# An attention kernel on one core: constants made between the evictions of x, and a tail whose banks are waited for singly

## The chip, the cores and the metric

The kernel runs on one core of one Trainium2 chip. A core has a matrix engine (TensorE; PE in the profile, PEld for its weight loads), a vector engine (VectorE, DVE), an activation engine (ScalarE, ACT), a general engine (GpSimd, POOL), a queue engine that here only issues DMAs (SyncE, SP), and 16 DMA engines. Each engine works through its own list of instructions in order, and waits on semaphores for the others. TensorE writes its results to PSUM, a memory of eight banks of 128 x 512 fp32; an "eviction" is the instruction that copies such a result to SBUF, the working memory.

The metric is the time of one execution on the device, in microseconds (us), taken as the median of several runs.

## The reference

Two attentions over the same x (1 x 2048 x 640, bf16) are mixed by a gate. Each has its own weights, 32 heads of 20 columns, and its own output projection.

```python
q, k, v = (x @ wqkv) split into 3 x 32 heads x 20
# A: full attention
p = softmax(q @ k.T * 20 ** -0.5)          # 2048 x 2048 for each head
a = (p @ v) @ wo
# B: each position sees itself and 7 earlier ones, 2 apart
logits = (q[s] . k[s - 2 * w]) * 20 ** -0.5   for w in 0..7, masked where s - 2 * w < 0
b = (softmax(logits) . v[s - 2 * w]) @ wo_B
g = sigmoid((x * gate_w).sum(-1))
out = g * a + (1 - g) * b
```

The exponentials of A, 32 x 2048 x 2048, are the bulk of the work.

## The kernel before

**Tiling.** Heads are taken in fours ("q" counts 8 groups of four heads), positions of the query in four chunks of 512 ("qc"). A unit is one head, one block of 128 keys and 512 queries: TensorE multiplies a slice of `kT` with `qT` into one PSUM bank (L1731), ScalarE takes the exponential of two or three banks at once into `ebuf` (L1756), and TensorE multiplies that with v into the bank `obank` (L1801). Some units go to VectorE instead, which makes powers of two by integer arithmetic (L1745, L905). Beside this stream run generators for all else: projections of q, k, v for the later heads, attention B, the gate, the output projection ("fold").

**What sets the order.** The kernel's text is a planner. Every call `T(engine, cost, instruction, reads, writes)` puts one instruction at the end of that engine's list, notes what it must wait for from the buffers it reads and writes, and advances a modelled clock for that engine, `sch.avail`. A generator is given its turn when the modelled clocks and free banks allow it. So the order of the body depends on those modelled clocks; at the end of the head they are set to fixed numbers (L1548). When the list of every engine is complete the instructions are emitted with their semaphores.

**The head** (about the first 18 us) is written out by hand, in this order:

1. Constants: an iota on GpSimd (L518); on VectorE `idf`, the difference of column and row index (L523, in the tile `rB`), the identity (L524), zeroed tiles (L534 to L542). GpSimd clears `vA` and five `qT` tiles (L527, L544).
2. x comes in four blocks of 512 rows by DMA. `turn` (L1400) transposes a block on TensorE into PSUM. `x_out` evicts it to `xT`: ScalarE takes two fifths (L1413), VectorE three (L1416).
3. On GpSimd, `w_pad` (L598) spreads the first weights of k into `kvw` once they have landed, an iota (L1472) writes the input of a later mask, and `kt_fill` (L1465) fills `kT` for groups 1 to 3 with a pattern read from the two-element tile `ones2`. Then come the first weights of q (L598 into `WqP`) and one more fill.
4. `k_first` (L1423) projects the first four heads' k for a block of 512 positions into a bank; `k_max` (L1437, VectorE) takes the largest |k| of it, and `k_out` (L1444, ScalarE) evicts it. The fourth block is projected in two halves (L1497), has its maxima taken in two (L1514) and is evicted in one piece by ScalarE (L1525). From the maxima VectorE makes `KM` (in the tile `eB`, L1520).
5. The first q is projected in two halves (L1497). |q| of the first half is made by ScalarE (L1517), of the second by VectorE (L1522). A matmul of |q| with `KM` (L1531) adds an upper bound of the scores, and VectorE writes both halves of `qT` from PSUM (L1535, twice). Then the first scores can be multiplied.

The blocks are interleaved on each engine's list as the calls of the module's end part stand: turn 0, x_out 0, turn 1, x_out 1, k_first 0, turn 2, k_max 0, k_out 0, x_out 2, k_first 1, turn 3, k_max 1, x_out 3, k_out 1, k_first 2, k_max 2, then the halves.

**The generator `constants()`** makes, after the head and between evictions of v, the following on VectorE: `KMd`, a mask for sums of |k| (three instructions, L554, L555, L557, from the iota of L1472), and `Rep`, a matrix that adds up heads: a copy of the identity (L562) and six additions `Rep = (idf == shift) + Rep` (L565), each of which reads the SBUF tiles `idf` and `Rep` and waits for the one before. `Rep` is needed by attention B only, `KMd` by the bounds of later heads.

**The tail** (`tail()`) is written by hand too. For the last 512 rows, four blocks of 128, part of the output projection has been summed up ahead. Columns 512 to 639 of all four blocks lie in a bank called the strip; columns 0 to 511 of blocks 2 and 3 in two "tail banks", those of blocks 0 and 1 in the two halves of `score[0]`. The last head's matmuls (L1212) go to the strip, block 2, block 3, block 0, block 1. VectorE adds the strip to what was summed before (L1234), ScalarE evicts blocks 2 and 3 (L1240), VectorE adds blocks 0 and 1 (L1243), and each block is written to memory by one DMA (L1248), those of blocks 2 and 3 issued from ScalarE, those of 0 and 1 from SyncE.

## Time and profile before

| | |
|---|---|
| median of 3 runs | 790.83 us (790.80 to 791.33) |
| profiled execution | 791.24 us, span of its instructions 789.4 us |
| TensorE clock granted | 1.000 |
| ScalarE busy in the span | 769.0 us (97%) |
| TensorE busy | 752.3 us (95%) |
| VectorE busy | 721.5 us (91%) |
| GpSimd busy | 123.9 us (16%) |
| first exponential begins | 18.22 us |
| busy before 18.2 us | TensorE 15.79, VectorE 13.45, GpSimd 9.81, ScalarE 8.39 us |
| busy from 784.5 us on | VectorE 1.88, ScalarE 1.09, TensorE 0.71 us |

The span runs from the first to the last instruction in the trace; the execution's time has 1.84 us more around it. A row of the page reads: line of the kernel, engine, operation, output tile <- input tiles, shapes, how often; after the bar the busy time, the mean duration in ns of one, and the idle time of the engine just before these instructions, with what ended that idle time. In the rows in order of time the first two columns are start and duration in us, and the bracket at the end is idle time before, with what ended it. Where several of one kind follow each other they share a row, "x3".

### The profile page before, as it was taken

What the parts mean: (1) busy time and instruction counts of PE and PEld (TensorE: products, weight loads), DVE (VectorE), ACT (ScalarE), POOL (GpSimd) and SP (SyncE); (2) the same over time, 40 slices, a digit from 0 to 9 for tenths busy, and PEclk for the clock granted to TensorE, in tenths of its full rate; (3) what the DMA queues carried; (4) which work ended last, traced back from release to release, by engine and by line L of the source; (5) the groups of instructions that cost most, each with busy time, mean ns of one, the idle gap of its engine ahead of it and who ended that gap; (6) DMA issues with size and microseconds to landing.
All of it is one profiled execution on the core that took longest, in us unless ns stands there. A gap on an engine that the chain in (4) does not pass through costs nothing.

```text
span 789.4 us, 29584 instructions
## 1 busy us (share of the span) xinstructions
PE 752.3 (95%) x12556; PEld 290.6 (37%) x12556; DVE 721.5 (91%) x1282; ACT 769.0 (97%) x732; POOL 123.9 (16%) x230
## 2 busy tenths in 40 slices
PE   8999999999999999999999999999999999999997
PEld 5423333232233334333334433434443433344323
DVE  7798888999999989999988999998999999898894
ACT  4999999999999999999999999999999999999996
POOL 4011202111112011111111101111111111111210
PEclk9999999999999999999999999999999999999999
DMA  7241121010021123130111312012113013100311
GB/s 227 62 109 25 40 44 33 14 24 18 8 71 30 41 42 73 24 72 16 23 40 42 76 41 58 14 41 71 25 31 71 26 24 71 46 7 7 74 31 40
DMA packets 62663, 36.16 MB, mean 46 GB/s; under 512 B 26884, under 2 KB 61972, under 8 KB 62532
## 3 DMA queue, kind: packets, MB, share of 16 engines
q1 hardware_dynamic: 62244, 33.94, 17.9%
q8 instruction: 100, 1.64, 0.9%
q10 hardware_dynamic: 288, 0.33, 0.1%
q14 instruction: 31, 0.25, 0.1%
HBM read 12.85 MB, written 3.54 MB: 21 GB/s over the span
## 4 chain that ended last, share of the span: by engine, by line
PE 43%; ACT 26%; DVE 17%; issue 11%; SPq 2%; DMA 1%; POOL 0%; DVEq 0%; ACTq 0%
ACT ebuf L1756 25%; PE score L1731 13%; PE obank L1801 12%; PE side L632 12%; DVE uD L1745 6%; DVE eD L905 4%; PE score L632 2%; DVE kvw L1092 1%; SPq L975 1%; DVE qkvB L967 1%; DMA oTd<-in_A_x_dram 1%; PE obank L1822 1%; PE score L1822 1%; PE side L1003 1%; DVE kvw L993 1%
## 5 line engine op out<-in xcount | busy, mean ns | idle before, releaser
L1756 ACT ACTIVATE ebuf<-score 128x1024 bf16<-128x1024 f32 (+1 forms) x699 | 757.0, 1266 | 4.4 <-PE score L1731 3.7
L1745 DVE TENSOR_SCALAR uD<-score 128x512 int16<-128x512 f32 x392 | 260.2, 680 | 14.7 <-PE score L1731 13.3
L1731 PE MATMUL score<-qT,kT 32*128 32x512 bf16 x1856 | 253.8, 384 | 17.7 <-ACT ebuf L1756 13.6
L905 DVE TENSOR_SCALAR eD<-uD 128x2048 int16<-128x2048 int16 x294 | 195.0, 687 | 4.5 <-PE obank L1801 3.4
L1801 PE MATMUL obank<-ebuf,vA 128*21 128x512 bf16 x1656 | 153.5, 385 | 1.7 <-DVE oTt L865 0.6
L1731 PEld LDWEIGHTS score<-qT,kT 32*128 32x128 bf16 x1856 | 63.0, 91 | 211.6 <-ACT ebuf L1756 147.4
L925 POOL TENSOR_TENSOR vS<-vA,vw 128x252 bf16<-128x252 bf16 x98 | 59.9, 613 | 388.5 <-DVE eD L905 252.8
L1801 PE MATMUL obank<-eD,vS 128*21 128x512 bf16 x1176 | 103.5, 379 | 0.0
L632 PE MATMUL side<-xT,wBs 128*32 128x256 bf16 x2400 | 93.6, 280 | 2.2 <-DVE oB L1125 0.7
L632 PEld LDWEIGHTS side<-xT,wBs 128*32 128x32 bf16 x2400 | 68.1, 141 | 27.9 <-issue 14.5
L1801 PEld LDWEIGHTS obank<-ebuf,vA 128*21 128x21 bf16 x1656 | 36.0, 89 | 83.0 <-issue 56.4
L1092 DVE TENSOR_TENSOR kvw<-kvw,eB 128x2048 bf16<-128x2048 bf16 x40 | 48.1, 1214 | 0.2 <-DMA kvw<-qkvB 0.2
L993 DVE TENSOR_TENSOR kvw<-qkvB 128x2048 bf16<-128x2048 bf16 x40 | 48.0, 1215 | 0.1
L882 POOL TENSOR_TENSOR oN<-oTt,rcp 128x256 bf16<-128x256 f32 x62 | 38.8, 625 | 58.0 <-DVE eD L905 39.5
L967 DVE CAST qkvB<-side 128x512 bf16<-128x512 f32 (+1 forms) x72 | 42.0, 593 | 4.5 <-PE side L632 4.3
L873 POOL TENSOR_TENSOR rcp<-rcp,gA 128x16 f32<-128x16 f32 x31 | 9.1, 292 | 192.0 <-DVE eD L905 90.9
L1801 PE MATMUL obank<-uD,vA 128*21 128x512 bf16 x392 | 38.1, 379 | 0.0
L1801 PEld LDWEIGHTS obank<-eD,vS 128*21 128x21 bf16 x1176 | 28.8, 91 | 19.8 <-issue 2.0
L1731 PE MATMUL score<-woBp,kT 32*128 32x512 bf16 x192 | 30.0, 384 | 1.8 <-ACT ebuf L1756 1.6
L632 PE MATMUL side<-xT,kvw 128*32 128x512 bf16 (+1 forms) x360 | 30.1, 382 | 0.6 <-DVE vA L833 0.3
L632 PE MATMUL side<-kvw,xT 128*32 128x160 bf16 (+1 forms) x740 | 28.5, 263 | 1.3 <-DVE vA L833 0.5
L865 DVE STREAM_TRANSPOSE oTt<-obank 128x512 f32<-128x512 f32 x32 | 22.6, 707 | 6.5 <-PE obank L1801 6.5
(194 smaller groups left out, 555.8 us busy)
## 6 DMA issues: line engine op xcount, KB each, us to landing
kvw<-qkvB SPq DMA_DIRECT2D x128, 80.6 KB
wBs<-in_B_wqkv_dram SPq DMA_DIRECT2D x15, 160.0 KB
WqP<-in_A_wqkv_dram SPq DMA_DIRECT2D x14, 160.0 KB
oTd<-oN SPq DMA_DIRECT2D x108, 20.0 KB
out_dram<-outsb SPq DMA_DIRECT2D x12, 160.0 KB
qT<-dst SPq DMA_DIRECT2D x93, 20.0 KB
kvw<-in_A_wqkv_dram SPq DMA_DIRECT2D x2, 800.0 KB
oTd<-in_A_x_dram SPq DMA_DIRECT2D x2, 640.0 KB
```

Of the source, the lines that this page charges most:

```text
L632: ins = e.matmul(o[j:k, :], l(j) if callable(l) else l[:, j:k], r, start=(first and i == 0), stop=(last and i == n - 1), skip_group_check= ...
L865: T("dve", 0.625, lambda e: e.transpose(oTt[:, :], obank[:, :]), reads=["obank"], writes=["oTt"])
L882: T(en, c2 if n == 4 else 0.56, lambda e, oo=oo, ii=ii, ib=ib: e.tensor_tensor(oo, ii, ib, ALU.mult), reads=["rcp", "oTt"], **{"accum" if ...
L905: T("dve", 0.065 + 0.1334 * n, lambda e, k=k, sl=sl: e.tensor_scalar(eD[:, sl % NS, 0:512 * n].bitcast(I16), uD[d % 2][:, 0:512 * n].bitca ...
L925: T("pool", 0.607, lambda e: e.tensor_tensor(vS[:, d % 2, :, :], _ap(vA, (kb * NQ + q) * 4 * DV, [[0, K - 1], [1, 4 * DV]]), _ap(vw, 0, [[ ...
L967: t = TB(dvc(n * TOK), lambda e, o=o, i=i: e.tensor_copy(o, i), reads=[("side", b)], writes=[key])
L993: TB(dvc(CH, 2), lambda e: e.tensor_tensor(o, i0, i1, ALU.mult), reads=["qB", "kB"], writes=[("prod", i)] + (["WkA", "WvA", ("WkP", 0)] if ...
L1092: TB(dvc(CH, 2), lambda e: e.tensor_tensor(o, i0, i1, ALU.mult), reads=["eB"] + [("vR", w4) for w4 in range(4)], writes=[("prod", i)], por ...
L1731: ins = e.matmul(o, kT[32 * j:32 * j + 32, q, kb * P:(kb + 1) * P], qT[qbuf[g]][32 * j:32 * j + 32, :], start=True, stop=True)
L1745: t = T("dve", 0.598, lambda e: e.tensor_scalar(uD[d % 2][:, 512 * i:512 * (i + 1)].bitcast(I16), side[x], UOFF, 0.0, op0=ALU.add, op1=ALU ...
L1756: exps[s] = T("act", actc(512 * n), lambda e: e.activation(ebuf[s % NE][:, 0:512 * n], score[s % 2][:, 0:512 * n], ACTF.Exp, scale=LN2 / S ...
L1801: ins = e.matmul(obank[32 * j:32 * j + DV, :], v, src, start=(kb == 0), stop=(last and k >= len(lst) - 4), skip_group_check=True)
```

## The change

It has four parts.

1. **`KMd` and `Rep` in the head.** The iota of L1472 goes on GpSimd ahead of the first weight copy, and the three instructions for `KMd` ahead of the first `turn`. The copy and the first three additions of `Rep` go behind the first `x_out`, the other three behind `k_max(0)`, `k_max(1)` and ahead of `k_max(2)`. In `constants()`, the generator's place is kept, but it only advances the modelled clock of VectorE (`gap`) by what the instructions took, so that the planner sees the same clocks as before.
2. **The last block of k is evicted in two halves** by ScalarE, the first ahead of |q|.
3. **The second half of the first `qT`** is written by ScalarE in place of VectorE.
4. **The tail's last matmuls** go to block 2, block 0, block 3, block 1, and each half of `score[0]` has its own semaphore value, so that block 0's addition waits for block 0 alone.

On the lists of TensorE, ScalarE, GpSimd and SyncE nothing else differs; on VectorE's list the additions are gone from between the evictions of v, and all that follows is in the same order.

```diff
-    def constants():
+    def kmd_const():
...
+    def rep_const(*shifts):
+        for sft in shifts:
             T("dve", 0.3, lambda e, sft=sft: e.scalar_tensor_tensor(
                 Rep[:, :], idf[:, :], float(sft), Rep[:, :], op0=ALU.is_equal, op1=ALU.add),
               reads=["rB", "Rep"], writes=["Rep"])
+
+    def constants():
+        last = [0.0]
+
+        def gap(d, dep=True):
+            last[0] = sch.avail["dve"] = max(sch.avail["dve"], last[0] + PAIR["dve", "dve"] if dep else 0.0) + d
...
-        for blk in (2, 3):
-            b = tail_bank[blk]
-            mm(("side", b), fold_mms(side[b][:, :], blk, q, 0, 512, False), True)
-        for blk in range(2):
-            mm(("score", 0), fold_mms(half(blk), blk, q, 0, 512, False), True)
+        for h in range(2):
+            b = tail_bank[2 + h]
+            mm(("side", b), fold_mms(side[b][:, :], 2 + h, q, 0, 512, False), True)
+            mm(("hb", h), fold_mms(half(h), h, q, 0, 512, False), True)
...
-              reads=[("score", 0), ("pre", blk)], writes=[("tout", blk)])
+              reads=[("hb", blk), ("pre", blk)], writes=[("tout", blk)])
...
+    T("pool", 0.4, lambda e: e.iota(itmp2[:, :], [[P, CN], [-DH, 32]], base=0, channel_multiplier=1), writes=[("outsb", 0, 0)])
+    kmd_const()
     turn(0)
     x_out(0)
+    T("dve", 0.1, lambda e: e.tensor_copy(Rep[:, :], ident[:, :]), reads=["ident"], writes=["Rep"])
+    rep_const(-96, -64, -32)
     T("pool", 0.55, w_pad(kvw, WKP_OFF, ebuf[3], 0, 4 * DH, 0), reads=[("ebuf", 3), "WkP"], writes=[("WkP", 0)])
-    T("pool", 0.4, lambda e: e.iota(itmp2[:, :], [[P, CN], [-DH, 32]], base=0, channel_multiplier=1), writes=[("outsb", 0, 0)])
...
     k_max(0)
+    rep_const(32)
     k_out(0)
...
     k_max(1)
+    rep_const(64)
     x_out(3)
     k_out(1)
     k_first(2)
+    rep_const(96)
     k_max(2)
...
+    def k3_out(h):
+        return T("act", actc(256), lambda e: e.activation(
+            kT[:, 0, 1536 + 256 * h:1792 + 256 * h], k3(h), ACTF.Identity, bias=onesrow[:, 0:1]),
+          reads=[("K3", h), ("score", 1), "onesrow", ("kmx4", 3 + h)], **{"accum" if h else "writes": [("kT", 0, 3)]})
+
+    k3_out(0)
     T("act", actc(256), lambda e: e.activation(qabs[0][:, 0:256], q0[0], ACTF.Abs), reads=[("Q0", 0)], writes=[("qabs", 0)])
+    t = k3_out(1)
...
-        t = T("dve", dvc(256), lambda e, h=h: e.tensor_scalar(
-            qT[0][:, hcols(h)], q0[h], OCT, offs[:, 0:1], op0=ALU.mult, op1=ALU.add),
+        if h == 0:
+            fn = lambda e: e.tensor_scalar(qT[0][:, hcols(0)], q0[0], OCT, offs[:, 0:1], op0=ALU.mult, op1=ALU.add)
+        else:
+            fn = lambda e: e.activation(qT[0][:, hcols(1)], q0[1], ACTF.Identity, scale=OCT, bias=offs[:, 0:1])
...
-    sch.avail.update(pe=17.6032304, dve=18.2962528, act=16.4994312)
+    sch.avail.update(pe=17.6032304, dve=18.2962528, act=16.4994312, pool=14.25)
```

25 lines of the change are left out of this document (13 added, 12 removed).

## The prediction, made before the change was run

> **What bounds the kernel now.** I read the busy table and the slices first, then the instructions of the head (the first 18 us) in order of time, then the rows where VectorE and GpSimd disturb each other, and last the writes at the end.
>
> ```profile
> PE 752.3 (95%) x12556; PEld 290.6 (37%) x12556; DVE 721.5 (91%) x1282; ACT 769.0 (97%) x732; POOL 123.9 (16%) x230
> ...
> ACT  4999999999999999999999999999999999999996
> ...
> L1756 ACT ACTIVATE ebuf<-score 128x1024 bf16<-128x1024 f32 (+1 forms) x699 | 757.0, 1266 | 4.4 <-PE score L1731 3.7
> ```
>
> From its first exponential on, ScalarE is the bound: 699 exponentials are busy for 757.0 us and it idles 4.4 us before them, half of that before the first two. So whatever moves the first exponential (18.22 us) moves the end by as much; nothing later has slack to give back. What is changed lies in the first 24 us and the last 5, so these decide.
>
> ```profile
> 6.60 0.96 DVE L1416 COPY xT<-score 128x1536 bf16<-128x1536 bf16 x1 [1.12 <-PE score L1400]
> 8.53 0.96 DVE L1416 COPY xT<-score 128x1536 bf16<-128x1536 bf16 x1 [0.98 <-PE score L1400]
> 9.61 0.69 DVE L1437 TENSOR_REDUCE kmx<-side 128x1 f32<-128x512 f32 x1
> 10.76 0.96 DVE L1416 COPY xT<-score 128x1536 bf16<-128x1536 bf16 x1 [0.46 <-PE score L1400]
> ```
> ```profile
> 7.64 0.52 POOL L598 COPY kvw<-ebuf 128x400 bf16<-128x400 bf16 x1 [2.89 <-DMA ebuf<-in_A_wqkv_dram]
> 8.10 0.27 POOL L1472 IOTA outsb<- 128x160 int32 x1
> 8.32 3.00 POOL L1465 COPY kT<-ones 128x1024 f32<-128x1024 f32 x3
> 11.84 0.53 POOL L598 COPY WqP<-ebuf 128x400 bf16<-128x400 bf16 x1 [0.53 <-DMA ebuf<-in_A_wqkv_dram]
> ```
>
> VectorE (first block) has gaps of 0.98, 0.46 and 0.43 us between the evictions of x, and the six additions to Rep are moved into them. But in the same microseconds GpSimd (second block) copies without a pause: the weight copy, then three fills of kT of about 1 us each. The reader should lay the two blocks over each other: every gap that the change fills, except the last two, has a GpSimd copy beside it. Before, the additions ran at 19.5 to 23.7 us, when GpSimd did nothing.
>
> ```profile
> 570.34 0.62 POOL L882 TENSOR_TENSOR oN<-oTt,rcp 128x256 bf16<-128x256 f32 x1 [1.03 <-DVE qabs L767]
> ...
> 572.11 0.61 POOL L925 TENSOR_TENSOR vS<-vA,vw 128x252 bf16<-128x252 bf16 x1 [1.16 <-DVE kvw L1092]
> 572.66 0.71 POOL L954 COPY qkvB<-qkvB 128x80 bf16<-128x80 bf16 x1
> ```
> ```profile
> 570.77 1.26 DVE L1092 TENSOR_TENSOR kvw<-kvw,eB 128x2048 bf16<-128x2048 bf16 x1
> ...
> 572.32 0.95 DVE L905 TENSOR_SCALAR eD<-uD 128x2048 int16<-128x2048 int16 x1
> ```
> ```profile
> 377.03 1.13 POOL L873 TENSOR_TENSOR rcp<-rcp,gA 128x16 f32<-128x16 f32 x1 [7.45 <-DVE kvw L1092]
> ```
>
> These rows show the two engines excluding each other. At 377.03 a GpSimd operation that takes 0.22 (median of 31) takes 1.13: it ends 0.07 after the VectorE product of two SBUF tiles (L1092) beside it. At 572.32 VectorE's shift, 0.69 otherwise, takes 0.95: it ends 0.55 after GpSimd's L925 (572.72). At 570.77 a product with two SBUF inputs ends 1.07 after GpSimd's L882 (570.96), 1.26 in place of 1.21. So a held VectorE operation needs, once the other has ended, its own time less about 0.145. Evictions from PSUM are not held: all four of L1416 take 0.96, three of them beside GpSimd copies.
>
> **The change, part by part.**
>
> *Three mask operations (L554, L555, L557) before the first eviction of x.* They took from 17.87 to 18.75, 0.88. Now VectorE is free at 5.47 and the first eviction begins at 6.60; 5.47 + 0.88 - 0.08 (an operation without a wait begins about 0.08 before the previous ends) = 6.27. The iota they need follows GpSimd's memsets, which end at 4.74, so about 5.0. Cost 0; the cover is 0.33 of idle time, and GpSimd is idle until 7.64.
>
> *Rep's copy and three additions between evictions one and two.* An addition (L565) takes 0.286 alone and reads two SBUF tiles (idf and Rep); each waits for the one before. The eviction ends at 7.56, the copy at 7.66. The first addition meets the weight copy (7.64 to 8.16) and is held: it ends 0.286 - 0.145 = 0.14 later, 8.30. The fill of kT that was queued takes the turn while the next addition waits for its semaphore: 8.30 to 9.28 (three take 3.00, 0.98 from one to the next). Second addition 9.42; second fill to 10.40; third addition 10.54. Queued behind it on VectorE is the second eviction of x, 0.87 more: 11.41 instead of 9.49, +1.92. TensorE's second projection of k waits for it, and so does the bank for the fourth turn of x.
>
> From there VectorE runs without gaps. The maximum of k's first bank ends at 12.02 (+0.61); the addition after it is held by the second weight copy (to 12.37) and ends at 12.51; eviction three 13.38; maximum 13.99; the fifth addition 14.19, beside memsets only; eviction four 15.06, where before it was 13.91. Its old gaps repay 0.8. The other queues are not later: TensorE's second projection starts at 11.47 and the turn of the fourth x block follows 1.07 later, ready for eviction at 13.86; ScalarE evicts k's first bank to 12.74 and x to 13.66 and 14.88. So k's last projection, which began at 14.03 behind ScalarE's 13.98, begins at 15.12: +1.09. The sixth addition costs 0.20 before the third maximum (15.87), which is free until k's halves arrive, 0.77 and 1.29 after their projection's start as before, at 15.90 and 16.41. I carry +1.08.
>
> For the write-only memsets the row is the one at 758.29, where a GpSimd memset took its usual 0.36 inside a VectorE product of 1.21: no hold. The Trainium skill's page "SBUF — State Buffer", section "Who interferes with whom", says the same of both kinds: a VectorE instruction with two SBUF inputs contends with a GpSimd instruction that reads SBUF, not with one that only writes, and the first to start keeps the shared port pair for its whole length. That rule speaks against this change; by it the sum is the one made here, and without it the first rival's.
>
> *k's last eviction in two halves, one ahead of |q|.* Two ScalarE operations of 0.38 (L1517's size) for one of 0.68: +0.09 on ScalarE, and |q|'s first half now stands behind the maximum of k's first half. That ends at 16.4, so |q| is ready near 17.2, and the bound matrix (16.37 before) at 17.45. Cost 0; the cover is 0.25, beyond which it would cost one for one.
>
> *The second half of the first q on ScalarE.* On VectorE it began at 17.24 and ended at 17.73, behind the first half. At 0.38 from 17.24, ScalarE ends at 17.62: -0.10. Behind its wait on ScalarE stands only the first exponential, which needs it anyway.
>
> *VectorE freed after the head.* Between 17.9 and 23.7 it loses ten operations. They stood ahead of evictions of v: one (18.69) began behind a mask operation ending 18.75, one (19.70) behind an addition ending 19.79, and the second exponential waited 0.85 for matmuls behind these. From 0 to -0.13; I take the middle, -0.06. Later additions lie beside gapless exponentials: 0.
>
> *The tail's banks waited for singly.* VectorE's last two additions no longer wait for both halves: the first began at 785.26, and can follow the strip's (ending 785.09), so both end 0.25 earlier.
>
> ```profile
> 786.00:787.00 1.00, 0.00 (x0) 0.00 (x0) 0.55 (x1) 0.00 (x0) 0.00 (x0) 1.00 0.85 298
> 787.00:788.00 1.00, 0.00 (x0) 0.00 (x0) 0.00 (x0) 0.00 (x0) 0.00 (x0) 1.00 0.98 348
> 788.00:789.40 1.40, 0.00 (x0) 0.00 (x0) 0.00 (x0) 0.00 (x0) 0.00 (x0) 1.00 0.02 6
> ```
>
> The last two columns are the DMA engines' share and GB/s. The four writes, 0.655 MB, keep the engines at 0.98 until they end, and the train starts with ScalarE's two, which do not move. From -0.14 (0.655 MB at 348 GB/s, 1.88 us from the first packet, against some 2.0) to 0; I take 0.
>
> Sum: +1.08 - 0.10 - 0.06 = **+0.92 us**. The profiled execution (791.24, span 789.4 and 1.84 around it) becomes 792.16; it stands 0.41 above the median of the three runs, so from 790.83 I predict **791.75**, +0.12%.
>
> **The rivals.**
>
> *No hold (the other side: faster).* If an addition is not held by a kT fill, copy and additions end at 7.66 + 3 x 0.325 = 8.63 and the second eviction at 9.50 against 9.49; the other three fit in their gaps. Then only -0.10 and -0.06 remain: 790.67, or 790.4 with the best of the tail and of freed VectorE. For it: the row at 570.77 is longer by only 0.05, and a fill reads a single repeated word. Against it: it ends just one stream after the GpSimd operation, as the one at 572.32 does. It decides if the second eviction ends before about 9.8.
>
> *GpSimd takes a second turn.* If a fill follows another while an addition waits, that is 0.98 more, with no gap left to repay it: +1.90, 792.73; two such turns use up the fills and give 792.9. For it: at 2.95 a GpSimd memset ran right behind another although a VectorE cast (L523, 2.57 us long) had waited since 1.10. Against it: at 572.66 a GpSimd copy queued 0.06 before L925's end, as the fills are, let VectorE's waiting shift go first (it took 0.71 for 0.25). It decides with 0.66 us of further hold, where the sum passes 1.58.
>
> *The change does not do what it says.* On each engine the order after the head is the same in both kernels, so a replanned body is excluded.
>
> **How the numbers follow.** Holding in turns 0.68, no hold 0.12, a second turn 0.18, something unseen 0.02. A measurement of this kernel tells about 0.2%, 1.58 us, from no change. The first two cases lie within it (0.80), the third above (0.18); faster than that needs something unseen (0.02). The range goes from no hold at its best, 790.4, to two second turns, 792.9; the likeliest case alone, with its unknown costs, spans 791.3 to 792.2.
>
> **What would show it.** Right: in the first stretch between evictions the second and third additions take about 1 us each and end 0.14 after a GpSimd copy; the second eviction ends near 11.4; the first exponential begins near 19.2; the write train lasts as long as before. Wrong: additions of 0.29 beside the fills and a second eviction at 8.6; two fills back to back with an addition waiting; a first exponential before 18.3 or after 19.8; or ScalarE idling longer in the body, which this account does not foresee.

## The result, and the profile after

The changed kernel took 793.56 us in the median of seven runs (792.62 to 795.56); the kernel before, beside it, 791.22 (790.55 to 791.34). The ratio is 1.0035, 95% interval 1.0026 to 1.0044: slower by 2 to 3.5 us. That is above the predicted range (790.4 to 792.9), and outside the 0.2% that was given a chance of 0.80. Part of the distance lies in the base: the prediction started from 790.83, the median of three runs, and the seven beside the changed kernel gave 791.22. Later series of the same kernel, on other chips, gave ratios of 1.0019 and 1.0014 (e1 and e9 below).

The profiled execution took 792.76 us, 1.52 more than the profiled one of before. 1.01 of it lies in the span (790.46 against 789.45), the other 0.51 in the time around it. First the row of the exponentials from the page of the changed kernel: busy time and mean are close to what they were (757.0 us, 1266 ns), and less idle time stands before them than before (4.4).

```profile
PE 752.1 (95%) x12556; PEld 290.7 (37%) x12556; DVE 722.5 (91%) x1281; ACT 769.9 (97%) x734; POOL 124.1 (16%) x230
...
L1781 ACT ACTIVATE ebuf<-score 128x1024 bf16<-128x1024 f32 (+1 forms) x699 | 757.2, 1263 | 3.7 <-PE score L1756 3.0
```

So the exponentials did not get slower; they begin later, at 18.90 in place of 18.22. Here is the first one, in the profile before and in that of the changed kernel:

```profile
18.22 1.45 ACT L1756 ACTIVATE ebuf<-score 128x1536 bf16<-128x1536 f32 x1 [1.37 <-PE score L1731]
```
```profile
18.90 1.45 ACT L1781 ACTIVATE ebuf<-score 128x1536 bf16<-128x1536 f32 x1 [0.58 <-PE score L1756]
```

VectorE and GpSimd of the changed kernel in the head, in order of time (start, duration):

```profile
6.51 0.96 DVE L1429 COPY xT<-score 128x1536 bf16<-128x1536 bf16 x1 [0.25 <-PE score L1413]
7.38 0.18 DVE L1486 COPY Rep<-ident 128x128 bf16<-128x128 bf16 x1
7.60 2.62 DVE L561 SCALAR_TENSOR_TENSOR Rep<-rB,Rep 128x128 bf16<-128x128 f32 x3
10.15 0.94 DVE L1429 COPY xT<-score 128x1536 bf16<-128x1536 bf16 x1
11.02 0.67 DVE L1450 TENSOR_REDUCE kmx<-side 128x1 f32<-128x512 f32 x1
11.62 0.27 DVE L561 SCALAR_TENSOR_TENSOR Rep<-rB,Rep 128x128 bf16<-128x128 f32 x1
```
```profile
7.48 0.52 POOL L612 COPY kvw<-ebuf 128x400 bf16<-128x400 bf16 x1 [2.52 <-DMA ebuf<-in_A_wqkv_dram]
7.94 3.18 POOL L1478 COPY kT<-ones 128x1024 f32<-128x1024 f32 x3
11.70 0.57 POOL L612 COPY WqP<-ebuf 128x400 bf16<-128x400 bf16 x1 [0.57 <-DMA ebuf<-in_A_wqkv_dram]
```

Three additions, 0.29 each when nothing disturbs them, take 2.62 us beside the fills of kT. One by one they take 0.54 (beside the weight copy, which ends at 8.00), 1.01 and 1.00; the second ends at 9.185, 0.14 after the first fill (9.046), the third at 10.224, 0.14 after the second (10.085). The hold in turns is there as predicted. The second eviction of x begins at 10.15 in place of 8.53, and the bound of k (L1544) at 16.41 in place of 15.81.

The last piece is the end. Stretches of the changed kernel (width, then busy time of PE, PEld, DVE, ACT and POOL, clock, DMA share, GB/s):

```profile
786.00:787.00 1.00, 0.22 (x5) 0.00 (x0) 1.00 (x3) 0.71 (x2) 0.00 (x0) 1.00 0.00 0
787.00:788.00 1.00, 0.00 (x0) 0.00 (x0) 0.29 (x1) 0.00 (x0) 0.00 (x0) 1.00 0.86 294
```

VectorE's last two additions follow the strip's without a gap, and measured from the strip's they are 0.27 us earlier than before, near the planned 0.25. But from the first issue of a write to the last landing it is 3.2 us in both kernels.

### The profile page after: what moved, and what is told of

The parts are those of the page before. It is cut to its first block, busy times and chain, and to the rows that moved or that the text cites. A ratio compares the mean times of both kernels' runs of the same rounds, so it can differ in the third digit from the quotient of the medians.

```text
span 790.5 us, 29588 instructions
## 1 busy us (share of the span) xinstructions
PE 752.1 (95%) x12556; PEld 290.7 (37%) x12556; DVE 722.5 (91%) x1281; ACT 769.9 (97%) x734; POOL 124.1 (16%) x230
## 4 chain that ended last, share of the span: by engine, by line
PE 43%; ACT 27%; DVE 18%; issue 10%; SPq 0%; DMA 0%; POOL 0%; DVEq 0%; ACTq 0%
ACT ebuf L1781 26%; PE score L1756 13%; PE obank L1826 12%; PE side L646 11%; DVE uD L1770 6%; DVE eD L919 4%; PE score L646 2%; DVE qkvB L981 1%; DVE kvw L1106 1%; DVE kvw L1007 1%; DVE vA L847 1%; PE obank L1847 1%; PE score L1847 1%; PE side L1017 1%; PE obank L529 1%
```

## The experiments

**A measure for all of them.** Every kernel here, unless its text says otherwise, computes the same output. What is compared is, first, the start of the first exponential; then the length of the body, from the start of the first exponential to that of the last; and the end, from there to the end of the span. Before: 18.22, 761.92 and 9.31. The first profile of the change: 18.90, 762.15 and 9.41.

### The change again, and its parts

Unaltered, on another chip:

> The changed kernel once more, unaltered. Three theories of its 2.3 us (median 793.56 against 791.22): the hold (VectorE's additions to Rep stand behind GpSimd's fills, and the head is 0.7 us late, as in the one execution seen: first exponential 18.90 instead of 18.22); a second turn of GpSimd in the other executions (head 1 us later still); and the body, where SyncE's issues of 0.71 us now and then take 1.6, twice ahead of the 43rd exponential in the execution seen. Hold alone: median 791.9, first exponential 18.9. Second turn: median 793.5, and in an execution of 793.5 or more the first exponential at 19.8 or later, with two fills back to back while an addition waits. Body: median 793.5 with the first exponential still at 18.9, and ScalarE idle for 1 us or more in the body.

792.16 us (791.29 to 793.74) against 790.92 for before, which is the base of e1 to e4; ratio 1.0019 [1.0009, 1.0030]. The eight executions fall into two groups, 791.29 to 791.64 and 792.68 to 793.74. The profiled one is of the earlier group (791.47): its first eviction began at 6.38, the additions took 0.29, 0.49, 1.01, 0.64, 0.58, 0.28, and the first exponential began at 18.57, only 0.35 late. Here the first addition began together with the weight copy (7.47) and kept its 0.29; the copy took 0.67 in place of 0.52, so the hold goes either way, and the fills came 0.14 us later.

Fills of `kT` moved behind the third maximum, on GpSimd alone:

```diff
-    for q in range(1, NQ):
-        if q == 4:
-            T("pool", 0.55, w_pad(WqP, 0, ebuf[4], 0, 4 * DH, 0, P), reads=[("ebuf", 4)], writes=WQ)
-        if q < 5:
-            kt_fill(q)
+    T("pool", 0.55, w_pad(WqP, 0, ebuf[4], 0, 4 * DH, 0, P), reads=[("ebuf", 4)], writes=WQ)
...
     k_max(2)
+    for q in range(1, 5):
+        kt_fill(q, [("kmx4", 2)])
```

> The changed kernel, but GpSimd's four fills of kT wait for the third maximum of k (the last addition to Rep is done by then), and the weight copy for q comes before them; the VectorE list is unchanged. Hold: additions take 0.29 again, all but the first, which still meets the weight copy for k (0.55); second eviction of x begins near 8.7 instead of 10.15, first exponential 18.3 to 18.4, time 790.9 to 791.4. Second turn: as hold, 791.2, since no fill is left to take a turn. If the constants cost by their mere place on VectorE's list, the first exponential stays at 18.9 and the time at 793.5. Body by chance of phase: time anywhere from 790.5 to 793 with the first exponential at 18.3.

791.48 us (790.87 to 791.72 and one of 795.66), ratio 1.0011 [1.0000, 1.0021]. All six additions took 0.28 to 0.29, and the bound of k began at 15.73, earlier than before's 15.81. The first exponential still came at 18.54, because the fills now met another operation: the product that writes `KM` (L1544 there) took 0.74 in place of 0.26.

The kernel before with a memset of VectorE ahead of the bound of k:

```diff
+    T("dve", 0.6, lambda e: e.memset(eD[:, 0, 0:1320].bitcast(FP32), 0.0), writes=[("eD", 0)])
     T("dve", 0.1, lambda e: e.tensor_scalar(kmx[:, 0:1], kmx[:, 0:1], kmx4[:, 3:4], kmx4[:, 4:5], op0=ALU.max, op1=ALU.max),
```

> The kernel before with one thing added: a VectorE memset of 660 words of an unused tile, 0.67 us, between the last maxima of k and the instruction that joins them, so that the first exponential is as late as in the changed kernel (18.9) and nothing else differs. Hold alone, where a later head is passed on one for one: 791.9. Body: a later head alone brings the long issues of SyncE onto the path, 793 to 794 with ScalarE idle for over 1 us in the body. Second turn: 791.9, for GpSimd and VectorE do not meet here.

791.26 us (790.73 to 791.71 and one of 793.52), 1.0008 [0.9999, 1.0016]. Of the memset's 0.61 us only 0.14 reached the first exponential (18.36): k's maxima had ended 0.17 us earlier than in before's profile (15.60 against 15.77), and the bound behind the memset took 0.10 in place of 0.27. So it says little about what a late head costs; e13 does that better.

Parts 2 to 4 without the constants:

```diff
-    kmd_const()
-    T("dve", 0.1, lambda e: e.tensor_copy(Rep[:, :], ident[:, :]), reads=["ident"], writes=["Rep"])
-    rep_const(-96, -64, -32)
...
-    rep_const(32)
...
-    rep_const(64)
...
-    rep_const(96)
```

(`constants()` is that of before.)

> The changed kernel with its first part undone: mask and Rep are made in the generator between the evictions of v, as before. Left are the fourth block of k in two evictions, the second half of the first q on ScalarE, and the tail's banks waited for singly. By the profile of the changed kernel ScalarE's half takes 0.475 and not 0.384, so the first exponential comes at 18.3 (before: 18.22) instead of 18.1, and the tail gives nothing: time 791.3 by every theory of the constants. If one of these parts costs the 2.3 us, it stays at 793.5.

791.95 us, 1.0012 [1.0003, 1.0021]. The first exponential began at 18.09, but its end is 10.48 us after the last exponential's start, 1.1 more than in the kernels so far; this is taken up below.

The tail alone put into before:

```diff
-        for blk in (2, 3):
...
+        for h in range(2):
+            b = tail_bank[2 + h]
+            mm(("side", b), fold_mms(side[b][:, :], 2 + h, q, 0, 512, False), True)
+            mm(("hb", h), fold_mms(half(h), h, q, 0, 512, False), True)
...
-              reads=[("score", 0), ("pre", blk)], writes=[("tout", blk)])
+              reads=[("hb", blk), ("pre", blk)], writes=[("tout", blk)])
```

> The kernel before with the tail's part alone: matmuls to block 2, 0, 3, 1 and block 0's addition waiting for block 0 only. Write train: the four writes take 3.25 us from the first issue to the last landing, as in six executions seen (3.24 to 3.26 in five of them, with either tail), so 790.9, no change. Late last write: since SyncE's first write now goes out at the same time as ScalarE's second (786.72 and 786.74 in the changed kernel, 786.0 behind 785.7 before), the two trains mix, and the last landing is often late by up to 1 us, as in the execution seen without the constants (4.32 us); then 791.6 to 791.9, and most of what that kernel lost.

790.49 us (790.15 to 791.10) against 791.52, ratio 0.9985 [0.9972, 0.9998]. The end is 9.39, so nothing was gained there; the body of the profiled execution is 760.94, 1.0 shorter than before's. Several of before's executions in this series were near 794 to 795, which widens the interval, and the gain is not one of the tail itself.

Parts 1 to 3 (the diff of e5 taken back from the changed kernel):

> The changed kernel with the tail's part undone. If the late last write carries some 0.7 us of the loss: 791.4 where the whole change gave 792.2. If the hold in the head carries all: 792.2, with the first exponential 12.2 to 12.4 us behind the first eviction of x (11.62 before).

792.12 us (790.98 to 794.18), 1.0006 [0.9994, 1.0019]; additions of 0.51, 1.01, 1.00, first exponential at 18.88.

Parts 2 and 3 alone (e4 with the tail of before):

> The kernel before with ScalarE's part alone: k's fourth block in two evictions, the second half of the first q on ScalarE. From the executions seen the first exponential is 0.13 later against the first eviction of x (11.75 and 11.62): 791.05. If this part carries the 1.0 us that the three parts without the constants lost: 791.9, and then the loss must show as idle time of ScalarE in the body, since the head's 0.13 can't hold it.

792.04 us (791.61 to 793.38), 1.0003 [0.9990, 1.0016]; first exponential at 18.06, end 10.46. In this and in e4 the half of `qT` on ScalarE took 0.47 us, where 0.38 had been assumed.

Part 1 alone (e6 with the last block of k evicted in one piece and the whole first `qT` on VectorE):

> The kernel before with the first part alone: mask and Rep in the head, all else as before. Hold, passed on one for one: the first exponential 12.1 to 12.3 us behind the first eviction of x and a time of 791.4 to 791.6. If the parts' losses add up, this one, ScalarE's and the tail's should give together the whole change's 1.2 us.

792.65 us (791.58 to 795.71), 1.0011 [0.9997, 1.0026]; additions of 0.49, 1.00, 1.01, first exponential at 18.77, end 10.38. Its profiled execution took 795.71 and has gaps of 1.87 and 1.18 us on ScalarE where before has 0.28 and 0.37. VectorE of this execution shows what ended them:

```profile
671.77 1.51 DVE L1765 TENSOR_SCALAR uD<-score 128x512 int16<-128x512 f32 x2
675.88 0.44 DVE L899 STREAM_TRANSPOSE oN<-oN 128x256 f32<-128x256 f32 x1 [2.60 <-DMA oTd<-oN]
676.25 0.65 DVE L1765 TENSOR_SCALAR uD<-score 128x512 int16<-128x512 f32 x1
```

The transpose may overwrite `oN` only when the DMAs that read it are done. Their last packets ended at 672.90, and VectorE was released 3.0 us after that; in before it was 1.2 (672.56 to 673.75). In both an instruction packet of 16 KB lies between, from 673.56 for 1.22 us here and from 673.51 for 0.92 there, so the packet alone does not tell them apart. The first gap is this wait. For the second, look at TensorE in the same microseconds (width, then busy time of PE, PEld, DVE, ACT and POOL, clock, DMA share, GB/s):

```profile
676.00:677.00 1.00, 0.00 (x0) 0.00 (x0) 0.97 (x3) 0.00 (x0) 0.00 (x0) 1.00 0.10 21
678.00:679.00 1.00, 1.00 (x12) 0.16 (x4) 1.00 (x3) 0.50 (x1) 0.61 (x2) 0.50 0.19 41
682.00:683.00 1.00, 1.00 (x23) 0.26 (x15) 0.78 (x2) 1.00 (x1) 0.00 (x0) 1.00 0.09 21
```

TensorE ran dry at 675.03 and began again at 677.04. From 677.78 on its granted clock was 0.50, for 3.41 us; four matmuls with v together took 0.65 us there, where they take 0.39 at the full clock, and the second gap of ScalarE lies in this stretch. In no other of the 20 profiles does the clock fall while TensorE still has work.

What these eight say together: where the constants are in the head and the fills where they were, the additions are held and the first exponential is 0.35 to 0.68 late; without constants, or with the fills late, no fill holds them. But the medians do not add up: taken alone the parts cost 1.1, 0.5 and -1.0 us, with intervals of about 1 us, and the change as a whole had cost 2.3 and 1.2. Nor are these prices of the parts alone: e7 and e8 (and e4) have the microsecond at the end in their profiles, which the whole change has not.

### How the head begins, and whether the executions differ by it

The next series looked at the change a third time, and shifted TensorE's instruction stream against the work, by cutting nine warm-up matmuls of 512 columns into 36 of 128:

```diff
-    warm_up = lambda e: e.matmul(obank[:, :], qabs[0][:, 0:P], qabs[0][:, :], start=True, stop=True)
-    for i in range(9):
+    warm_up = lambda e: e.matmul(obank[:, 0:P], qabs[0][:, 0:P], qabs[0][:, 0:P], start=True, stop=True)
+    for i in range(36):
```

> The changed kernel once more, unaltered, beside the next two, to see what its later executions are made of. Theory (instruction fetches): the head comes late by the 0.6 to 0.7 us already seen (first exponential 12.2 to 12.4 us after the first eviction, against 11.6), and whatever the execution has above 791.5 us stands in a few gaps of ScalarE in the body (0.5 to 1.9 us each, near the 43rd and the 606th exponential) or in the last write's landing (1.05 us late), each with an instruction packet beside it; time 791.3 to 794.0. Rival (GpSimd takes a second turn in the later executions): the fourth addition would take over 0.5 us and the first exponential would come 13 us or more after the first eviction, with a body without such gaps.

792.17 us (791.01 to 793.22), 1.0014 [1.0004, 1.0023]. Its ten executions spread without two clear groups; the profiled one (792.71) lies in the upper half, and looks otherwise than the theory said. VectorE of e9 in the head:

```profile
7.09 0.96 DVE L1429 COPY xT<-score 128x1536 bf16<-128x1536 bf16 x1 [0.82 <-PE score L1413]
7.96 0.18 DVE L1486 COPY Rep<-ident 128x128 bf16<-128x128 bf16 x1
8.18 3.09 DVE L561 SCALAR_TENSOR_TENSOR Rep<-rB,Rep 128x128 bf16<-128x128 f32 x3
11.20 0.94 DVE L1429 COPY xT<-score 128x1536 bf16<-128x1536 bf16 x1
```

The first eviction begins 0.58 later than in the first profile of the change. GpSimd is where it was (weight copy at 7.50, fills from 7.95), so now all three additions meet fills, 1.01 each, still strictly in turns; the fourth meets the second weight copy (0.69). The bound of k begins at 17.78, and the first exponential at 20.27: 2.05 late, and 13.18 after the first eviction, with no gap like e8's behind it. These are the signs named for the rival, but not its cause: no two fills follow each other while an addition waits. Why the first eviction was later is seen on TensorE, in the transposes of the first block of x. The first profile of the change and then e9, stretches of 0.5 us, operations of L1413 alone (width, busy time and count of PE and PEld, clock, DMA share, GB/s):

```profile
5.00:5.50 0.50, 0.43 (x6) 0.44 (x7) 1.00 1.06 379
5.50:6.00 0.50, 0.50 (x13) 0.50 (x11) 1.00 1.08 366
6.00:6.50 0.50, 0.47 (x9) 0.30 (x6) 1.00 1.22 257
6.50:7.00 0.50, 0.00 (x0) 0.00 (x0) 1.00 1.22 273
```
```profile
5.00:5.50 0.50, 0.42 (x5) 0.42 (x6) 1.00 1.07 376
5.50:6.00 0.50, 0.50 (x7) 0.50 (x6) 1.00 1.08 367
6.00:6.50 0.50, 0.50 (x8) 0.50 (x6) 1.00 1.22 254
6.50:7.00 0.50, 0.50 (x9) 0.37 (x6) 1.00 1.18 268
```

The reader should look at the counts: from 5.5 to 6.0 e9 issues 7 transposes where the first profile has 13, and it is done half a microsecond later. The spacing of two transposes falls from 0.107 to 0.056 us at 5.4 us in the first profile of the change, at 6.6 in e9, and is 0.056 nearly from the first transpose on (5.1) in e1. The granted clock column shows 1.00 in all these rows, so in them only the spacing tells; but the trace's record of the clock begins at just these times, 5.34, 6.54 and 4.95 us. The Trainium skill, page "TensorE: Matmul & The Clock Gate", part 1 on the clock gate, has the two spacings (106.7 and 55.6 ns at 128 columns) and says that the switch to the full clock waits for a busy window that runs freely against the kernel's start, and so comes at a varying time, by ±500 ns. The traces agree in the spacings and in that it varies, but by more than that.

> The changed kernel with its nine warm-up matmuls of 512 columns cut into 36 of 128: as much warm-up work, 27 matmuls and 27 weight loads more in TensorE's stream, and every engine's order otherwise as before. The packets on the queue of TensorE's instructions are 100 of 16 KB, 1.638 MB for 25,594 records, 64 bytes a record; 54 records more are 3.4 KB, a fifth of a packet, so each fetch falls some 1.9 us earlier beside the same work (they come 8.5 to 9 us apart). Theory (a fetch that meets SyncE's issue or a transfer makes them late): the long issues at 50.4 and 57.3 and the gap at the 43rd exponential go or change size, other issues become long, and the time moves by 0.3 to 1.5 us against the unaltered change, in either sign; the head stays 0.6 to 0.7 late. Rival (the loss beyond the head comes from the later head itself, whatever the fetches do): the time stays within 0.3 us of the unaltered change, with the same long issues at the same places.

792.88 us (791.17 to 793.52), 1.0019 [1.0010, 1.0028]. The long issues did move (50.4 and 57.3 are gone, one is at 58.0). But the spacing fell only at 6.9 us, the first eviction began at 7.24, and the first exponential at 20.22 as in e9, so this run cannot tell the fetches' part from the head's.

> The kernel before with the same 36 short warm-up matmuls, nothing else. Theory (fetches): the same computation with its fetches some 1.9 us earlier beside the work: the long issues of SyncE lie at other places, and the time moves by 0.3 to 1.5 us against before, in either sign, though nothing on the path was changed. Rival (fetches cost nothing that matters at the end): within 0.2 us of before.

790.90 us (790.60 to 791.20) against 791.21, 0.9997 [0.9987, 1.0006]: no effect that can be told. On the whole time the rival was nearer. What it shows is something else. Here too the spacing fell late (6.7 us) and the first eviction began at 7.12, but the second began at 8.35 and the first exponential at 18.07. Before takes no harm from a late first eviction.

That makes a theory: the change turns the varying start of TensorE's full clock into a varying hold, in how many operations meet fills and for how long. Two kernels test it by forcing the late start with memsets of VectorE, TensorE left alone:

```diff
     turn(0)
+    T("dve", 0.0, lambda e: e.memset(eD[:, 0, 0:980].bitcast(FP32), 0.0), writes=[("eD", 0)])
+    T("dve", 0.0, lambda e: e.memset(eD[:, 0, 0:980].bitcast(FP32), 0.0), writes=[("eD", 0)])
     x_out(0)
```

> The changed kernel with two memsets of VectorE (128x490 words of a scratch buffer, about 0.46 us each by the 0.61 us for 660 words in e3_delay) behind the mask operations, so that the first eviction of x cannot begin before about 7.1 us in any execution. In the profiles so far it begins at 6.4 to 6.5 where TensorE reaches its short spacing of transposes (0.056 us) by 5.5 us, and at 7.1 to 7.2 where that comes at 6.6 or later. Theory (how many additions meet fills of kT depends on when the first eviction ends): three additions take about 1.0 us each, the second eviction begins at 11.2 to 11.4, the first exponential near 20.2 as in e9_after_third, 1.3 later than in the first profile of the changed kernel (18.90); the time is 792.2 to 793.6, without executions below 792. Rival (the first eviction's start is absorbed by the gaps behind it, and the two kinds of execution have another origin): the first exponential at 18.9 to 19.1 and the same spread of times as e9_after_third (791.0 to 793.2).

792.81 us (792.40 to 793.67) against 790.95, 1.0024 [1.0013, 1.0035]. The spacing fell early (by 5.1 us), the first eviction was kept back to 7.34, and the head is that of e9. VectorE of e13:

```profile
7.34 0.89 DVE L1429 COPY xT<-score 128x1536 bf16<-128x1536 bf16 x1
8.15 0.87 DVE L1488 COPY Rep<-ident 128x128 bf16<-128x128 bf16 x1
9.06 2.41 DVE L561 SCALAR_TENSOR_TENSOR Rep<-rB,Rep 128x128 bf16<-128x128 f32 x3
11.38 0.95 DVE L1429 COPY xT<-score 128x1536 bf16<-128x1536 bf16 x1
```

It is now the copy and two additions that wait for the three fills (0.87, 1.04, 1.01); the third addition finds no fill left (0.29). The first exponential begins at 20.25. No execution of the seven is below 792.4: the earlier group is gone.

> The kernel before with two such memsets (920 and 840 words, about 1.65 us together, since VectorE is free from 5.5 us here), so that its first eviction begins at about 7.1 too. Theory: before has 0.98 us of idle VectorE behind its first eviction, in which a late start disappears: the second eviction still begins at 8.3 to 8.7, the first exponential at 18.0 to 18.4, the time within 0.3 us of before. Rival (a late first eviction costs any kernel the same): first exponential 18.8 or later, time 0.4 us or more above before.

790.81 us (790.54 to 792.01), ratio 1.0000 [0.9991, 1.0009] (the edit is that of e13, with memsets of 920 and 780 words). VectorE of e14:

```profile
7.30 0.90 DVE L1416 COPY xT<-score 128x1536 bf16<-128x1536 bf16 x1
8.38 0.96 DVE L1416 COPY xT<-score 128x1536 bf16<-128x1536 bf16 x1 [0.18 <-PE score L1400]
9.57 0.69 DVE L1437 TENSOR_REDUCE kmx<-side 128x1 f32<-128x512 f32 x1 [0.24 <-PE side L1423]
```

0.7 us of lateness went into the gap ahead of the second eviction (0.18 is left of 0.98), and the first exponential began at 18.15. The same late start costs before nothing and the changed kernel 1.35 us of head against its first profile.

Last, the fills made by a memset, which writes the same word and reads nothing:

```diff
-        T("pool", 0.95, lambda e: e.tensor_copy(
-            kT[:, q, :].bitcast(FP32), _ap(ones2, 0, [[0, S // 2], [1, 2]]).bitcast(FP32)),
-          reads=["ones2"], writes=[("kTz", q)])
+        T("pool", 0.95, lambda e: e.memset(kT[:, q, :].bitcast(FP32), 1.0019378662109375), writes=[("kTz", q)])
```

> The changed kernel with the fills of kT made by a GpSimd memset of the same word (1.0019378662109375 in f32, two bf16 ones) in place of a copy that reads the ones from SBUF; same places, same order. Theory (only GpSimd operations that read SBUF hold VectorE's additions): the additions take 0.28 to 0.30 except those beside the weight copies (0.3 to 0.7), the first exponential comes at 18.2 to 18.6 whichever way TensorE starts, and the times lose their upper group: 790.9 to 791.8. Rival (any GpSimd operation holds them): additions of 1.0 beside the memsets, 791.0 to 793.3 as in e9_after_third.

VectorE, then GpSimd, of e16 in the head:

```profile
7.64 1.16 DVE L561 SCALAR_TENSOR_TENSOR Rep<-rB,Rep 128x128 bf16<-128x128 f32 x3
8.71 0.95 DVE L1429 COPY xT<-score 128x1536 bf16<-128x1536 bf16 x1
```
```profile
7.48 0.52 POOL L612 COPY kvw<-ebuf 128x400 bf16<-128x400 bf16 x1 [2.51 <-DMA ebuf<-in_A_wqkv_dram]
7.94 2.73 POOL L1478 MEMSET kT<- 128x1024 f32 x3
```

The three additions take 1.16 together in the same place, the first 0.50 beside the weight copy, the others 0.29 beside memsets. The first exponential begins at 18.13. So a fill that only writes does not hold them; the fill that also reads does. The profiled execution took 790.69; but the median of ten was 792.11 (790.69 to 794.47), 1.0013 [1.0003, 1.0023]. The expectation for the time was missed: the later executions stayed although no fill held an addition in the profile. Two more runs asked why:

> e16_fill_memset again, unaltered: its profile was the fastest of its ten executions (790.69), while the others reached 794.47. Theory (with the hold gone, what is left of the spread is made in the body): in a slower execution the first exponential still comes at 18.0 to 18.5, and the time above 791 stands in one or two gaps of ScalarE of 0.5 us or more that the first profile does not have, each with a late transfer on SyncE's queue. Rival (the hold comes back in some executions): additions of 1.0 and a first exponential of 19 or later.

793.23 us (790.64 to 795.10) on another chip, 1.0030 [1.0017, 1.0043]. The profiled execution was again an early one (790.68, first exponential at 18.13), so the later ones were not seen from inside. One thing is on record of them: the four of 794.17 and more have a mean granted clock of 0.997 or 0.998, the other six 0.999 or 1.000.

e18 is e16 with the last block of k evicted and the first q's second half made as in before, and one more small memset:

```diff
     T("dve", 0.1, lambda e: e.memset(zero[:, :], 0.0), writes=["zero"])
+    T("dve", 0.0, lambda e: e.memset(zero[:, :], 0.0), writes=["zero"])
```

> The changed kernel with memset fills, without the parts on ScalarE, and with one more memset of 16 words on VectorE in the start: the records of VectorE's stream are as many as in e15_late_no_act_1 and in before (1473), and ScalarE's as before (1443 in place of 1448). Theory (the wide spread of e16 belongs to where the fetches fall in its longer ScalarE and shorter VectorE streams): 790.7 to 791.3 and a spread as narrow as e15's (most executions within 0.6 us). Rival (it belongs to the memset fills or to the constants in the head): 791.5 or more in the median, executions up to 793 and above.

791.23 us, 1.0009 [0.9996, 1.0021]; six of ten executions at 790.39 to 791.50, two at 793.83 and 794.33. These two have a mean clock of 0.998 and 0.997, the others 0.999 or 1.000. The median fits the theory, the two late ones do not. It stays open.

### The microsecond at the end

The profiles of e4, e7 and e8 end 10.4 to 10.5 us after the last exponential begins, the others 9.3 to 9.4, whichever tail they have. A fourth showed it: e12, which is e2 (the fills late) with parts 2 and 3 undone, so with the last block of k evicted in one piece and the whole first `qT` written by VectorE:

```diff
-            fn = lambda e: e.activation(qT[0][:, hcols(1)], q0[1], ACTF.Identity, scale=OCT, bias=offs[:, 0:1])
...
-    k3_out(0)
...
-    t = k3_out(1)
...
+    t = T("act", actc(512), lambda e: e.activation(kT[:, 0, 1536:2048].rearrange("p (h c) -> p h c", c=256),
+                                               _ap(score[1], 0, [[512, 2], [1, 256]]), ACTF.Identity, bias=onesrow[:, 0:1]),
```

> The changed kernel with GpSimd's four fills of kT behind the third maximum of |k|, so that they share no time with VectorE's additions, and with the first q's second half and the rows of the last k chunk evicted as before; the constants stay in the head, the tail waits singly. Theory (the hold is the head's loss, ScalarE's half costs 0.1 more): additions of 0.28 to 0.30 us, the first exponential 11.55 to 11.7 us after the first eviction, as before (11.62); time within 0.7 us of before, what is left being where the fetches fall. Rival (six additions in the head cost even unheld): first exponential 11.9 or later.

792.31 us (791.78 to 792.77), 1.0015 [1.0005, 1.0024]. The additions took 0.28 to 0.29 but the first, beside the weight copy (0.65). The first exponential began at 18.46, 12.14 after the first eviction and not 11.55 to 11.7. That is where the rival had put it, but not for its reason: the product for `KM` was held by the late fills as in e2 (0.74). The end is 10.50.

In the four kernels with the late end, and in no other of the 20 profiles, VectorE's stream has 1472 records in the trace; the others have 1471, or 1473 to 1475. An 8 KB instruction packet lies 8.06 to 8.17 us after the last exponential begins in those four, while the writes are on their way; with 1473 or more it lies at 3.7 to 3.8, with 1471 behind the end. So one record more was put in, a memset of 16 words in the first microseconds:

```diff
     T("dve", 0.1, lambda e: e.memset(zero[:, :], 0.0), writes=["zero"])
+    T("dve", 0.0, lambda e: e.memset(zero[:, :], 0.0), writes=["zero"])
```

> e12_late_no_act with one more memset of 16 words on VectorE in its start, which waits for nothing and nobody waits for. In all the profiles the last write lands 1.05 us late exactly where VectorE's stream has 1472 records in the trace (e4, e7, e8, e12), and not with 1471 or 1473; in those an 8 KB instruction packet lies 8.1 to 8.2 us after the last exponential begins, in the midst of the writes. Theory (it is that packet that holds the write): with 1473 records the packet comes some 4 us earlier, the end is 9.3 to 9.4 us after the last exponential's start in place of 10.50, and the time falls by about 1.0, to 791.1 to 791.5. Rival (the late landing has another cause and the count is chance): 10.4 to 10.5 again, 792.0 to 792.6.

791.12 us (790.67 to 792.42), 1.0005 [0.9995, 1.0014]: an instruction that does nothing made the kernel 1.2 us faster than e12, measured against the medians of before beside each 0.9. SyncE's waits in the last 10 us (in total, times, the longest), first of e12, then of e15:

```profile
SPq L351 <- DMA out_dram<-kvw: 2.8, 2, 1.7
```
```profile
SPq L351 <- DMA out_dram<-kvw: 1.7, 2, 1.1
```

That is one pair of kernels and one profile of each; with the packet's place in the other 18 it makes the packet the likely cause. The packets of data end 8.54 us after the last exponential begins in e12, 0.45 later than in the change's own profiles, and the semaphore of the last write follows 1.0 after them; in e15 it is 7.95 and 0.35. The end is 9.27.

## Why the prediction was wrong, and where it was right

**The masks ahead of the first eviction** cost nothing in the early executions, as said: VectorE waited 0.25 for TensorE before the first eviction.

**The hold in turns** was right as a mechanism: each held addition ended 0.14 after a fill, no fill took a second turn while an addition waited, and evictions from PSUM were not held. By the same measure "no hold" is out. The size, +1.08, was not right: in the first profile of the change the bound of k was 0.60 late, since the second eviction ended at 11.09 and not 11.41 and the fourth addition began at 11.62, before the weight copy (11.70). In e9, e10 and e13 it was 1.92 to 1.97 late.

The step that failed is the one that took the first eviction's end, 7.56, from one execution and laid all that follows over GpSimd's row. GpSimd's start is fixed by a DMA (7.41 to 7.50 in the profiles with these fills and the constants in the head), the first eviction's by TensorE's full clock, and ranged from 6.38 to 7.24 (e1 and e10). With it the first exponential went from 0.35 to 2.05 late. Before shows no such thing, because the gaps that the change filled were what took up that difference; the prediction counted them as free. How far this step carries the measured time is only partly shown. Forcing the late start makes every execution late (e13), but taking the hold away (e16, e17) did not take the late executions away, and the first series (793.56) lies above even the forced kernel (792.81).

**The second half of the first q on ScalarE** was put at -0.10. It took 0.475 (17.845 to 18.320) against VectorE's 0.48, and the first exponential followed 0.58 behind it, where it followed VectorE by 0.50. The term is about +0.1, as VectorE would have been free at the same time: from the bound of k to the first exponential it is 2.41 to 2.42 us in before, e5 and e18, which leave ScalarE's parts out, and 2.48 to 2.49 in e4, e7, e16 and e17, which have them.

**k's last eviction in two halves** (0.47 each, not 0.38) stayed under its cover: |q| was ready at 16.88, the bound matrix at 16.97.

**VectorE freed after the head** was put at -0.06 and is 0: the second exponential begins 2.30 after the first in both kernels.

**The tail** was put at 0 and is 0.

**"Nothing later has slack to give back"** was too simple. The bodies of the profiles last 760.9 to 762.4 us, with or without a late head (means 761.6 of six profiles in which fills held additions, 761.4 of thirteen without; e8's 764.6 left out). On average, then, a late head is passed on. In one execution it need not be: e9's first exponential was 2.05 late, its last 0.99; the first change's 0.68 and 0.91. The differences arise at a few places where ScalarE waits for a chain of DMAs. One is the exponential that begins at 67.56 in the first profile of the change (the 44th; the expectations call it the 43rd):

```profile
65.33 1.56 ACT L1781 ACTIVATE ebuf<-score 128x1536 bf16<-128x1536 f32 x1
67.56 1.02 ACT L1781 ACTIVATE ebuf<-score 128x1024 bf16<-128x1024 f32 x1 [0.67 <-PE score L1756]
```

TensorE waited 1.54 there for `woBp<-scr_q`, which SyncE issued 2.5 us later than in before, behind two issues of 1.60 and 1.58 us where 0.71 is usual. SyncE's row of the first of them (durations in ns, min, median, max), and the row of TensorE's instruction queue in two of its microseconds, 50 to 52:

```profile
L696 SPq DMA_DIRECT2D kT<-qkvB x3: 706/706/1602, 48.9 to 50.4; - x3
```
```profile
q8 instruction: 1, 0.02, 4.3%
```

This packet came at 50.2. The prediction saw none of this.

**The rivals.** "GpSimd takes a second turn" gave 792.73 to 792.9 by a hold of 0.66 or more beyond the forecast. That much hold came, in e9 and e10 unforced and in e13 forced, but from one more operation that met a fill or the second weight copy, not from two fills in a row. So its mechanism was not right, and that its price fits e9's 792.71 and e13's 792.81 is in part luck: in e9 the body was 1.06 us shorter than in before. "No hold" did not occur.

**What the runs do not settle.** A head that is 2.0 late, forced in every execution, gives 1.0024 (e13), an unforced mixture of early and late ones 1.0014 to 1.0019. The first series' 1.0035, and executions of 793.8 to 795.7 in several kernels (in before, six of 35 on one chip), contain something more. The only such execution that was profiled, e8's, has it in the body: a wait for a DMA's end of 3.0 us, and behind it 3.41 us at half the clock. Such a stretch takes 0.002 from the mean clock of an execution, and the record of the others shows it: of before's six late ones, five have 0.997 or 0.998 and one 1.000; e2's 795.66 has 0.995. (In e4, e7, e8 and e12 earlier executions have 0.998 too, so there it tells less.) So in most of the latest executions TensorE seems to have lost its full clock for a while; 795.56 in the first series (0.999) and 794.18 in e6 (1.000) are exceptions. It does not explain the first series, whose mean clocks are 0.999 and 1.000, nor the executions of 792 to 793.3 in e16 and e17. e16 and e17 have many late executions while no fill holds an addition in their profiles, e2 and e15 few. Whether the change makes them more frequent, and how, is open.

## What to carry to other kernels

An idle gap in one profile may be what takes up the jitter of something upstream: before filling it, ask what starts the instruction ahead of it, and how much that start varies against the engine beside it. A profile of one execution gives one draw of such a phase; where the cost jumps with the phase (one more operation meets one more fill), work out the early and the late case and predict the mixture. And if VectorE operations on SBUF must lie beside GpSimd work, let that work write without reading: a memset in place of a broadcast copy took the hold away here, though not the late executions. When executions of one kernel differ, look at the mean granted clock of each, to three digits, before looking for a cause in the order of the work.

## What the runs showed of the hardware that was not expected

- *Copies and scalings are held too.* Beside a fill, VectorE's copy of `Rep` from one SBUF tile (bf16) took 0.87 to 0.88 us in place of 0.18, and the product for `KM`, with one SBUF tile, 0.74 in place of 0.26. The prediction had reckoned only with two SBUF inputs. The Trainium skill, page "SBUF — State Buffer", section "Who interferes with whom", names such copies and scalings, when they run in a two-port mode, as taking the shared ports; the traces agree.
- *Instruction packets and SyncE.* In the 20 profiles of this case, 252 issues of SyncE after the first 15 us took more than 1.15 us (0.66 is the median). All 252 overlap in time with an instruction packet of 16 or 8 KB. But so do 106 to 122 more in each profile that are not long. That the packets cause it is argued from this coincidence; shifting them (e11) moved the long issues but not the time.
- *One instruction can be worth 1 us.* A record more or less in VectorE's stream decides whether an instruction packet falls into the final writes: e12 and e15 differ by one memset of 16 words, their ends by 1.23 us. The cause is argued from the packet's place.
- *The start of TensorE's full clock* varied from 4.17 (e14) to 6.88 us (e10) after the start of the span, by the trace's record of the clock, which begins there; the column of the stretches shows 1.00 before it too.
- *Half the clock in the middle of the work.* In e8 TensorE had nothing to do for 2.0 us (675.03 to 677.04), and from 677.78 its granted clock was 0.50 for 3.41 us. Whether the idle time brought it on, this one profile does not show.
